# Local attention's weighted sum by accumulating transfers instead of additions on Pool

## The chip, the cores and the metric

The kernel runs on one core of a Trainium2 chip. The core has five engines, each with an instruction queue of its own that runs in order: TensorE (PE), VectorE (DVE), ScalarE (ACT), GpSimd (called Pool here) and SyncE (SP), which in this kernel issues nearly all transfers. They wait for each other by semaphores. The metric is the time of one execution on the device in microseconds (us), median of several runs.

## The reference

The input `x` has 2048 positions of 448 channels, which are 16 heads of 28. Two attentions are computed from it and mixed by a gate per position:

```python
g = _sigmoid((x * gate_w).sum(-1, keepdims=True))
a = _A_ref(x, A_wqkv, A_wo)
b = _B_ref(x, B_wqkv, B_wo)
return g * a + (1 - g) * b
```

B is full softmax attention over all 2048 positions. A is local: each position looks at 8 positions (itself and those 2, 4, ... 14 before it):

```python
W, dil = 8, 2
logits = jnp.einsum("bhsd,bhswd->bhsw", q, kg) * scale
logits = jnp.where(mask[None, None, :, :], logits, -1e9)
attn = _softmax(logits, axis=-1)
o = jnp.einsum("bhsw,bhswd->bhsd", attn, vg)
```

Its last line, a sum of 8 weighted values, is what the change is about. Everything is float32.

## The kernel before

Three stages follow one another. **The projections** (to about 254 us) make queries, keys and values of both attentions and the gate. **The main loop** has 256 steps: 16 units of 16 steps, `st = 16 * u + kt`. A unit is four heads by 512 queries of attention B, a step is 128 of its keys. **The output products** with `wo` begin at step 236 between the last steps and run to the end.

A step of the main loop issues, on TensorE, the scores (line 1022, three products each for accuracy), up to three products for the maxima of a later unit (line 144, until step 234) and the weighted sum of the step before (line 976). ScalarE takes two exponentials (line 1025). VectorE takes two reductions for the maxima (line 148).

**Attention A lies beside this**, in 8 groups of two heads, on VectorE and above all on Pool. A tile is 128 partitions x 896 elements (16 positions x 56 channels), 448 KB. For group `c` and offset `w`:

- `a_score` (line 607): Pool multiplies `q` by the shifted `k` (line 611) into a tile `prod`, and in 40 of 64 cases adds its halves (line 616). `a_reduce` (line 619): VectorE sums each head of it (line 621).
- `a_softmax` (line 623): nine small operations on Pool, VectorE and ScalarE.
- `a_av` (line 653): part 0 multiplies the shifted `v` by the weights (line 661), for `w` = 0 straight into the sum `oat[c]`, else into a tile `prod`; part 1 adds that tile to `oat[c]` (line 666). After the last, `oat[c]` is stored to DRAM (line 669).

The tiles `prod` of scores and of sums come from one pool of five buffers (line 589).

**The order is a list made while the program is written.** `item` puts each operation in a list of its engine with a key (its rank), a cost in us, and needs, each an earlier operation and the number of steps it must lie back. At each step `issue` goes through the list of an engine by rank and issues what has its needs, until `late[eng] + cost` passes a limit, 4.2 us for Pool. `late` falls by 2.25 us a step (2.1 after the maxima end). The engines then run in that order and wait where data is missing. A cost that is too small makes the list issue more than the engine can do.

Other work on Pool is issued by step, not by the list:

- **Maxima.** When a unit's maxima are complete, `max_parts` (line 172) reduces them on VectorE (line 174), copies them on ScalarE and subtracts on Pool (`nmt`, line 181). Two steps later VectorE transposes the result (`nms`, line 186).
- **The end of a unit** (lines 905 to 918), counted from `f = 16 * (u + 1)`: `fin_copy` copies the sums out of PSUM (step f + 1); `fin_sum` and `fin_sum2` bring the softmax sums through DRAM (f + 1, f + 3); `fin_inv` takes the reciprocal on VectorE (line 844) and multiplies it on Pool (line 845, f + 6); `fin_spread` and `fin_spread2` spread it through DRAM as `rbc` (lines 849 and 854, f + 6 and f + 8); `fin_on` multiplies on Pool (line 883, f + 12); `fin_hi` rounds on ScalarE (line 887, f + 15); `fin_lo` subtracts on Pool (line 891, f + 16); `fin_store` stores (f + 19). `pool_time` adds the cost of `fin_on` and `fin_lo` to `late["pool"]`.

When all lists are empty and the last group is stored, `a_done` (line 761) loads `wo` into the room of attention A's tiles and splits it (line 759) over the next thirteen steps.

Of the kernel before, what the change touches and what calls it, by code (L numbers as in the profile page):

```python
# [11 lines left out]
ALU = mybir.AluOpType  # L12
# [8 lines left out]
NU = NG * NB  # L21
# [4 lines left out]
def gated_mix_kernel(ctx: ExitStack, tc: tile.TileContext, xT, xn, gw, wA, wB, woAB, out):  # L26
    nc = tc.nc
# [156 lines left out]
    def max_turn(t):  # L184
        r = sp.tile([128, 32], F32, name="nms")
        nc.vector.transpose(r, t)
        return r
# [18 lines left out]
    with tc.tile_pool(name="xp", bufs=1) as xp, tc.tile_pool(name="wp", bufs=2) as wp:  # L206
# [203 lines left out]
        r, t = xst[:, 0, 0:3, :], xst[:, 0, 3, :]  # L410
# [7 lines left out]
        for kt in range(3):  # L418
            nc.vector.tensor_tensor(out=xl[0][:, kt, :], in0=r[:, kt, :], in1=xh[0][:, kt, :].bitcast(F32),
                                    op=ALU.subtract)  # L420
        nc.vector.tensor_tensor(out=tail[64:128], in0=t[64:128], in1=tail[64:128].bitcast(F32), op=ALU.subtract)
        nc.vector.tensor_tensor(out=wl0[:, 3, 0:256], in0=wt0[:, 0:256], in1=wh0[:, 3, 0:256].bitcast(F32),
                                op=ALU.subtract)
# [27 lines left out]
        for n, t in enumerate(tiles):  # L451
# [4 lines left out]
            for w in splits:  # L456
                i, k = (n - splits[w][0]) * splits[w][1], splits[w][1]
# [36 lines left out]
            if parts and parts[0][0] <= n:  # L494
                _, u, t = parts.pop(0)
                max_store(u, max_turn(t.bitcast(F32)))
            if finished and n < len(tiles) - 3:
                u = finished.pop(0)
                parts.append((n + 3, u, max_parts(u)))
            if n == 64:  # L500
                gate = []
                for sgn, dst in ((-1.0, g_t), (1.0, omg)):
                    e = sp.tile([128, NJ], F32, name="ez")
# [5 lines left out]
            if n == 70:  # L509
                r = max_turn(omw)  # L510
# [10 lines left out]
    def at(pos, st, f):  # L521
        hooks.setdefault((st, pos), []).append(f)
# [12 lines left out]
    pool = ctx.enter_context(tc.tile_pool(name="psv", bufs=1, space=bass.MemoryType.PSUM))  # L535
# [55 lines left out]
    for nme in ("k", "v"):  # L591
        for i in range(2):
            t = a1.tile([128, HALO + NJ, 56], F32, name=f"{nme}t{i}")
            kvt[nme, i] = t
    qt, Lt, oat, lst, prods = {}, {}, {}, {}, {}
# [23 lines left out]
    def a_reduce(c, w, i, n):  # L619
        r = slice(2 * NJ // n * i, 2 * NJ // n * (i + 1))  # L620
        nc.vector.tensor_reduce(Lt[c][:, w].rearrange("p j h -> p (j h)")[:, r], prods[c, w][:, r], axis=X, op=ALU.add)
# [31 lines left out]
    def a_av(c, w, part):  # L653
        if part == 0:
            if w == 0:
                oat[c] = a2.tile([128, NJ, 56], F32, name="oat")
                dst = oat[c]
            else:
                dst = a3.tile([128, NJ, 56], F32, tag="prod", name="prod2")
            oat[c, w] = dst  # L660
            nc.gpsimd.tensor_tensor(  # L661
                out=dst.rearrange("p j (h d) -> p j h d", d=DH),
                in0=kvt["v", c % 2][:, HALO - DIL * w:HALO - DIL * w + NJ, :].rearrange("p j (h d) -> p j h d", d=DH),
                in1=Lt[c][:, w, :, :, None].to_broadcast([128, NJ, 2, DH]), op=ALU.mult)
        else:
            nc.gpsimd.tensor_tensor(out=oat[c], in0=oat[c], in1=oat[c, w], op=ALU.add)  # L666
            if w == W - 1:
                stored[0] = now[0] + 4
                at("end", stored[0], lambda: nc.sync.dma_start(oa_scr[:, :, 56 * c:56 * c + 56], oat[c]))


# [3 lines left out]
    now = [0]  # L675
    stored = [0]

    def item(eng, key, name, cost, needs, f):
        lists[eng].append((key, name, cost, needs, f))

    CH, NR = 21, {}
    for c in range(8):
        for w in range(W):
# [2 lines left out]
    for c in range(8):  # L686
        c0 = CH * c
        for nme in "qkv":
            item("sp", c0 if nme != "v" else c0 + 18, ("ld", nme, c), 0,
                 [(("s", c - 2, 7), 3)] if nme != "v" else [(("a", c - 2, 7, 1), 3)],  # L690
                 lambda c=c, nme=nme: a_load(c, nme))
        for w, o in enumerate((0, 2, 5, 8, 11, 14, 17, 20)):
            back = (c, w - 4) if w > 3 else (c - 1, w + 4)
            item("pool", c0 + o, ("s", c, w), 2.05 + 1.0 * (NR[c, w] == 2),
                 [(("ld", "k", c), 4), (("ld", "q", c), 4), (("a", c - 3, 7, 0), 0), (("s", c, w - 1), 0)]
                 + ([(last(*back), 0)] if back in NR else []), lambda c=c, w=w: a_score(c, w))
            for i in range(NR[c, w]):
                item("dve", c0 + o + 2 + 0.1 * i, ("r", c, w, i), 0.32,
                     [(("s", c, w), 3), (("r", c, w, i - 1) if i else last(c, w - 1) if w else ("r",), 0)],
                     lambda c=c, w=w, i=i: a_reduce(c, w, i, NR[c, w]))  # L700
        for i, (eng, o, cost, lag) in enumerate((("pool", 22, 0.68, 2), ("dve", 23, 0.35, 3), ("dve", 23.5, 0.35, 0),
                                                 ("pool", 25, 0.68, 1), ("act", 26, 0.3, 3), ("dve", 27, 0.35, 1),
                                                 ("dve", 27.5, 0.35, 0), ("dve", 27.8, 0.36, 0),
                                                 ("pool", 28, 0.9, 1))):
            item(eng, c0 + o, ("m", c, i), cost, [(last(c, 7) if i == 0 else ("m", c, i - 1), lag)],
                 lambda c=c, i=i: a_softmax(c, i))
        n = 0
        for w in range(W):
            for part in ((0,) if w == 0 else (0, 1)):
                item("pool", c0 + 30 + 1.4 * n, ("a", c, w, part), 1.65 if part == 0 else 2.05,  # L710
                     [(("m", c, 8), 0), (("ld", "v", c), 4),
                      (("a", c, w - 1, 1 if w > 1 else 0) if part == 0 else ("a", c, w, 0), 0)],
                     lambda c=c, w=w, part=part: a_av(c, w, part))
                n += 1
    for q in lists.values():
# [2 lines left out]
    late = {"pool": 0.0, "dve": 0.0}  # L718
# [109 lines left out]
    fin = {}  # L828
# [13 lines left out]
    def fin_inv(u):  # L842
        r = sp.tile([128, 16], F32, name="finv")
        nc.vector.reciprocal(r, fin["s"])
        nc.gpsimd.tensor_tensor(out=r, in0=r, in1=og[:, u % NB, :], op=ALU.mult)
        fin["rec"] = r
# [50 lines left out]
                r = 112 * g + DH * h  # L897
                dma_r(dst[r:r + DH, 512 * b:512 * b + 512], t[32 * h:32 * h + DH])

    def pool_time(f, *x):  # L900
        late["pool"] += 1.25
        f(*x)


    for u in range(NU - 1):
        f = NJ * (u + 1)
        l = {NU - 3: (1, 2, 5, 6, 9, 12, 13, 15), NU - 2: (1, 2, 5, 6, 8, 10, 10, 12)}.get(
            u, (1, 3, 6, 8, 12, 15, 16, 19))
        at("pre", f + 1, lambda u=u: fin_copy(u))
        at("end", f + l[0], lambda u=u: fin_sum(u))  # L910
        at("end", f + l[1], lambda u=u: fin_sum2(u))
        at("dve", f + l[2], lambda u=u: fin_inv(u))
        at("end", f + l[2], lambda u=u: fin_spread(u))
        at("end", f + l[3], lambda u=u: fin_spread2(u))
        at("end", f + l[4], lambda u=u: pool_time(fin_on, u, fin["r"]))
        at("pre", f + l[5], lambda u=u: fin_hi(u))
        at("end", f + l[6], lambda u=u: pool_time(fin_lo, u, nc.gpsimd))
        at("end", f + l[7], lambda u=u: fin_store(u))


# [20 lines left out]
    part = {}  # L941
# [108 lines left out]
    for u in range(NU):  # L1050
        g, b = divmod(u, NB)
        for kt in range(NJ):
            st = NJ * u + kt
            now[0] = st
            if kt == (8 if u < 12 else 12) and u + 1 < NU:
                load_q(u + 1)
            run("pre", st)
            issue("sp", st, 0)
            if st >= A_START:
                issue("pool", st, 4.2)  # L1060
            if not adone and not any(lists.values()) and st > stored[0]:
                a_done(st)
            cur = {}
            left = s1e - s1c[0]
            for a in scores(u, kt, cur):
                if a == 2:
                    run("mid", st)
            run("dve", st)
            if u and kt == 6:
                late["dve"] += 0.25  # L1070
            if finished:
                v = finished.pop(0)
                t = max_parts(v)
                late["dve"] += 0.3
                turned = {}
                lag = 2 if v < NU - 1 else 1
                at("dve", st + lag, lambda t=t, w=turned: w.update(r=max_turn(t.bitcast(F32))))
                at("end", st + lag, lambda v=v, w=turned: max_store(v, w["r"]))
            issue("dve", st, DLIM)
            issue("act", st, 0)  # L1080
            run("act", st)
            if prev is not None:
                do_av(prev)
            prev = (kt, cur, g)
            if OPS and st >= OPS[0]:
                op_some(st, 7)
            run("end", st)
            step = 2.25 if left else 2.1
            late["dve"] = max(0.0, late["dve"] + 0.58 * min(3, left) - step)
            late["pool"] = max(0.0, late["pool"] - step)  # L1090
            if st == OP0 + 31:
                op_load_b(2, 3)
            if not OPS and s1c[0] == s1e:
                s1_close()
                at("pre", st + 1, lambda: op_t(0))
                at("end", st + 1, lambda: op_split(0))
                OPS.append(st + 2)
# [61 lines left out]
```

## Time and profile before

| | us |
|---|---|
| median of 3 runs | 922.4 (921.13 to 923.32) |
| the profiled execution | 920.4 |
| its span, first to last instruction | 918.4 |
| busy: PE, DVE, ACT, POOL | 905.2, 731.7, 652.5, 620.8 |
| granted TensorE clock | 0.998 |

A row of a group of instructions gives the line, the engine, the operation, output and input tile, their shape, the count; then busy time in total and mean ns of one; then the idle time of the engine just before them and what ended it. A row of the timeline gives start and duration in us, then the instruction, with such an idle time in brackets. "SPq" is the queue of SP that issues transfers. A row of the stages gives start and end, length, the busy time of PE, its weight loads, DVE, ACT and POOL with counts, then clock, the share of the transfer engines, and GB/s.

### The profile page before, as it was taken

What the parts mean: (1) busy time and instruction counts of PE and PEld (TensorE: products, weight loads), DVE (VectorE), ACT (ScalarE), POOL (GpSimd) and SP (SyncE); (2) the same over time, 40 slices, a digit from 0 to 9 for tenths busy, and PEclk for the clock granted to TensorE, in tenths of its full rate; (3) what the DMA queues carried; (4) which work ended last, traced back from release to release, by engine and by line L of the source; (5) the groups of instructions that cost most, each with busy time, mean ns of one, the idle gap of its engine ahead of it and who ended that gap; (6) DMA issues with size and microseconds to landing.
All of it is one profiled execution on the core that took longest, in us unless ns stands there. A gap on an engine that the chain in (4) does not pass through costs nothing.

```text
span 918.4 us, 20670 instructions
## 1 busy us (share of the span) xinstructions
PE 905.2 (99%) x8396; PEld 541.2 (59%) x8396; DVE 731.7 (80%) x977; ACT 652.5 (71%) x802; POOL 620.8 (68%) x485
## 2 busy tenths in 40 slices
PE   8999999999999999999999999999999999999998
PEld 6899999999944444444344444343444444466667
DVE  6488999999989999999889999998999888500012
ACT  6456434433388889898788898888989889855551
POOL 2499746554479799998999999999994851300100
PEclk9999999999999999999999999999999999999999
DMA  9977403544374322235135241531412123453422
GB/s 266 294 254 201 127 11 103 154 120 113 81 245 117 86 81 88 69 91 131 33 117 136 81 102 44 140 93 25 111 44 53 34 63 103 147 161 110 138 82 97
DMA packets 101119, 104.30 MB, mean 114 GB/s; under 512 B 61652, under 2 KB 71252, under 8 KB 100240
## 3 DMA queue, kind: packets, MB, share of 16 engines
q1 hardware_dynamic: 100880, 102.72, 39.4%
q8 instruction: 66, 1.08, 0.5%
q10 hardware_dynamic: 144, 0.26, 0.2%
q14 instruction: 29, 0.24, 0.1%
HBM read 61.99 MB, written 40.48 MB: 112 GB/s over the span
## 4 chain that ended last, share of the span: by engine, by line
PE 76%; POOL 12%; SPq 4%; DMA 4%; ACT 2%; DVE 1%; issue 1%; POOLq 0%; ACTq 0%; DVEq 0%
PE T L1022 20%; PE av L976 18%; PE r L298 14%; PE T L815 8%; PE r L293 7%; PE r L144 5%; POOL prod L611 3%; POOL oat L666 3%; POOL prod L661 3%; SPq L101 2%; PE T L144 2%; DMA rbc<-rs 2%; ACT P L1025 1%; SPq L854 1%; DVE MX L148 1%
## 5 line engine op out<-in xcount | busy, mean ns | idle before, releaser
L1025 ACT ACTIVATE P<-T 128x1024 f32<-128x1024 f32 x512 | 497.2, 1024 | 85.2 <-PE T L1022 83.6
L148 DVE TENSOR_REDUCE MX<-T 128x1 f32<-128x512 f32 x470 | 441.1, 954 | 36.0 <-PE T L144 22.5
L976 PE MATMUL av<-P,V 128*32 128x512 f32 x2048 | 273.6, 606 | 0.0
L1022 PEld LDWEIGHTS T<-QH,KH 30*128 30x128 f32 x1024 | 90.9, 182 | 226.8 <-ACT P L1025 203.3
L144 PE MATMUL T<-KH,QP 28*128 28x512 f32 x704 | 219.3, 453 | 1.4 <-DVE MX L148 1.1
L1022 PE MATMUL T<-QH,KH 30*128 30x512 f32 x1024 | 212.0, 489 | 5.9 <-ACT P L1025 5.0
L162 DVE TENSOR_REDUCE MX<-r 128x2 f32<-128x1024 f32 x160 | 192.6, 1221 | 24.6 <-PE r L144 22.9
L1022 PE MATMUL T<-QH,KL 28*128 28x512 f32 x1024 | 186.5, 397 | 0.0
L1022 PE MATMUL T<-QL,KH 28*128 28x512 f32 x1024 | 184.1, 393 | 0.0
L611 POOL TENSOR_TENSOR prod<-qt,kt 128x896 f32<-128x896 f32 x64 | 135.0, 2113 | 1.4 <-DMA kt<-a_scr 1.4
L362 ACT ACTIVATE raw<-r 128x896 f32<-128x896 f32 (+1 forms) x64 | 58.9, 921 | 97.8 <-PE r L298 96.5
L666 POOL TENSOR_TENSOR oat<-oat,prod 128x896 f32<-128x896 f32 x56 | 118.1, 2109 | 2.3
L144 PEld LDWEIGHTS T<-KH,QP 28*128 28x128 f32 x704 | 86.2, 182 | 28.8 <-ACT P L1025 21.4
L661 POOL TENSOR_TENSOR prod<-vt,L 128x896 f32<-128x896 f32 x56 | 95.4, 1703 | 0.6
L363 POOL TENSOR_TENSOR ast<-raw 128x448 f32<-128x448 f32 x48 | 55.5, 1157 | 58.1 <-ACT raw L362 45.6
L1022 PEld LDWEIGHTS T<-QL,KH 28*128 28x128 f32 x1024 | 93.9, 185 | 0.0
L1022 PEld LDWEIGHTS T<-QH,KL 28*128 28x128 f32 x1024 | 92.2, 183 | 1.0
L144 PE MATMUL r<-KH,QP 64*128 64x512 f32 x320 | 86.7, 390 | 0.0
L976 PEld LDWEIGHTS av<-P,V 128*32 128x32 f32 x2048 | 40.3, 108 | 77.5 <-issue 72.4
L298 PE MATMUL r<-wh,xh 64*128 64x448 f32 (+1 forms) x512 | 85.4, 362 | 0.0
L803 DVE TENSOR_TENSOR oalo<-T,oah 128x384 fp32r<-128x384 f32 x16 | 8.9, 557 | 90.8 <-ACT onhi L802 82.2
L298 PE MATMUL r<-wh,xl 64*128 64x448 f32 (+1 forms) x384 | 70.0, 363 | 0.0
(110 smaller groups left out, 1112.9 us busy)
## 6 DMA issues: line engine op xcount, KB each, us to landing
a_scr<-ast SPq DMA_DIRECT2D x24, 448.0 KB
qk_hi<-qkh SPq DMA_DIRECT2D x24, 256.0 KB
qk_lo<-qkh SPq DMA_DIRECT2D x24, 256.0 KB
rbc<-rs SPq DMA_DIRECT2D x60, 64.0 KB
QP<-qk_hi SPq DMA_DIRECT2D x64, 56.0 KB
KL<-qk_lo SPq DMA_DIRECT2D x16, 224.0 KB
QH<-qk_hi SPq DMA_DIRECT2D x64, 56.0 KB
QL<-qk_lo SPq DMA_DIRECT2D x64, 56.0 KB
```

The lines of the kernel that those rows point to most:

```text
L144: nc.tensor.matmul(bank, qhis[u][h % 2][r, 128 * qs:128 * qs + 128], KH[u // NB % 3][r, 512 * kc:512 * kc + 512], start=True, stop=True)
L148: r = nc.vector.tensor_reduce(MX[:, n % NMX:n % NMX + k], bank, axis=X, op=ALU.max)
L162: nc.vector.tensor_reduce(m, PM[k], axis=X, op=ALU.max)
L293: nc.tensor.matmul(bank, ws[c][rows, k, t[4]:t[4] + 128], x, start=first, stop=last)
L298: nc.tensor.matmul(bank[:, 0:cols], x, ws[c][rows, k, 0:cols], start=first, stop=last)
L611: nc.gpsimd.tensor_tensor(out=p, in0=qt[c], in1=kvt["k", c % 2][:, HALO - DIL * w:HALO - DIL * w + NJ, :], op=ALU.mult)
L661: nc.gpsimd.tensor_tensor(out=dst.rearrange("p j (h d) -> p j h d", d=DH), in0=kvt["v", c % 2][:, HALO - DIL * w:HALO - DIL * w + NJ, :].r ...
L666: nc.gpsimd.tensor_tensor(out=oat[c], in0=oat[c], in1=oat[c, w], op=ALU.add)
L815: writes(bank, nc.tensor.matmul(bank[:, :D], src, wo[c][:, k, :], start=(first and k == ks[0] and i == 0), stop=(last and k == ks[-1] and ...
L976: nc.tensor.matmul(av[32 * h:32 * h + 32, :], V[:, kt, 4 * g + h, :], tiles_[h], start=(kt == 0), stop=(kt == NJ - 1), skip_group_check=True)
L1022: nc.tensor.matmul(bank[a], (KH[g % 3], KH[g % 3], KL[g % 2])[t][r, ks], (qh, ql, qh)[t][r, :], start=(t == 0), stop=(t == 2))
L1025: e = nc.scalar.activation(p, RP[0] if a == "2" else mine, AF.Exp, scale=SCALE).ins
```

## The change

Part 1 of `a_av` no longer adds on Pool: Pool issues a transfer that adds the tile to `oat[c]` on its way from SBUF to SBUF. There are 56 of them. The list gets other costs and needs: a product needs the one before it, and the sum four offsets back issued a step before; a transfer needs its product a step before and the transfer before it three steps before. The store of a group comes 6 steps after its last sum, not 4. `fin_hi`, `fin_lo` and `fin_store` of the first 11 units come three steps later. `finv` and `nmt` now count as Pool time.

```diff
-            nc.gpsimd.tensor_tensor(out=oat[c], in0=oat[c], in1=oat[c, w], op=ALU.add)
+            nc.gpsimd.dma_start(oat[c].rearrange("p j e -> p (j e)"), oat[c, w].rearrange("p j e -> p (j e)"),
+                                accum_op=ALU.add)
             if w == W - 1:
-                stored[0] = now[0] + 4
+                stored[0] = now[0] + 6
                 at("end", stored[0], lambda: nc.sync.dma_start(oa_scr[:, :, 56 * c:56 * c + 56], oat[c]))
...
+    ACC = 1.0
...
-            item("pool", c0 + o, ("s", c, w), 2.05 + 1.0 * (NR[c, w] == 2),
+            item("pool", c0 + o, ("s", c, w), 2.15 + 0.98 * (NR[c, w] == 2),
...
-        for i, (eng, o, cost, lag) in enumerate((("pool", 22, 0.68, 2), ("dve", 23, 0.35, 3), ("dve", 23.5, 0.35, 0),
-                                                 ("pool", 25, 0.68, 1), ("act", 26, 0.3, 3), ("dve", 27, 0.35, 1),
+        for i, (eng, o, cost, lag) in enumerate((("pool", 22, 0.69, 2), ("dve", 23, 0.35, 3), ("dve", 23.5, 0.35, 0),
+                                                 ("pool", 25, 0.69, 1), ("act", 26, 0.3, 3), ("dve", 27, 0.35, 1),
                                                  ("dve", 27.5, 0.35, 0), ("dve", 27.8, 0.36, 0),
-                                                 ("pool", 28, 0.9, 1))):
+                                                 ("pool", 28, 1.14, 1))):
...
-                item("pool", c0 + 30 + 1.4 * n, ("a", c, w, part), 1.65 if part == 0 else 2.05,
+                item("pool", c0 + 30 + 1.4 * n, ("a", c, w, part), 1.72 if part == 0 else ACC,
                      [(("m", c, 8), 0), (("ld", "v", c), 4),
-                      (("a", c, w - 1, 1 if w > 1 else 0) if part == 0 else ("a", c, w, 0), 0)],
+                      (("a", c, w - 1, 0), 0) if part == 0 else (("a", c, w, 0), 1),
+                      (("a", c, w - 4, 1), 1) if part == 0 else (("a", c, w - 1, 1), 3)],
...
-    def pool_time(f, *x):
-        late["pool"] += 1.25
+    def pool_time(t, f, *x):
+        late["pool"] += t
         f(*x)
...
-            u, (1, 3, 6, 8, 12, 15, 16, 19))
+            u, (1, 3, 6, 8, 12, 18, 19, 22) if u < NU - 5 else (1, 3, 6, 8, 12, 15, 16, 19))
...
-        at("dve", f + l[2], lambda u=u: fin_inv(u))
+        at("dve", f + l[2], lambda u=u: pool_time(0.18, fin_inv, u))
...
-        at("end", f + l[4], lambda u=u: pool_time(fin_on, u, fin["r"]))
+        at("end", f + l[4], lambda u=u: pool_time(1.24, fin_on, u, fin["r"]))
...
-        at("end", f + l[6], lambda u=u: pool_time(fin_lo, u, nc.gpsimd))
+        at("end", f + l[6], lambda u=u: pool_time(1.24, fin_lo, u, nc.gpsimd))
...
                 late["dve"] += 0.3
+                late["pool"] += 0.18
```

## The prediction

> **What bounds the kernel now.** I read the page's totals, its 40 slices and its chain first, then placed one instruction that occurs once per unit of 16 steps on the time axis, and then opened the worst stretch instruction by instruction.
>
> ```profile
> PE 905.2 (99%) x8396; PEld 541.2 (59%) x8396; DVE 731.7 (80%) x977; ACT 652.5 (71%) x802; POOL 620.8 (68%) x485
> POOL 2499746554479799998999999999994851300100
> PE 76%; POOL 12%; SPq 4%; DMA 4%; ACT 2%; DVE 1%; issue 1%; POOLq 0%; ACTq 0%; DVEq 0%
> ```
>
> TensorE is busy everywhere and carries the chain. Pool is saturated only in the middle of the span, and it is on the chain for 12%: not because its work is the longest, but because somebody waits for it somewhere. Where, the start of `fin_copy` shows. It is issued at step 1 of each unit; these four belong to steps 17, 65, 161 and 209.
>
> ```profile
> 292.01 0.60 ACT L831 ACTIVATE osb<-av 128x512 f32<-128x512 f32 x1
> 400.21 0.60 ACT L831 ACTIVATE osb<-av 128x512 f32<-128x512 f32 x1
> 625.86 0.60 ACT L831 ACTIVATE osb<-av 128x512 f32<-128x512 f32 x1
> 733.95 0.60 ACT L831 ACTIVATE osb<-av 128x512 f32<-128x512 f32 x1
> ```
>
> Steps 17 to 65 took 108.20 us, 161 to 209 took 108.09 us: 2.253 us a step, twice the same, although Pool adds in both. The 96 steps between took 225.65 us where 96 x 2.253 = 216.3 would do. **So 9.3 us are lost there, and that is all that a faster Pool can win in this loop**; the step itself is set by TensorE, VectorE and ScalarE. The worst of those units, first as Pool and VectorE see it:
>
> ```profile
> 448.06 0.26 DVE L174 TENSOR_REDUCE m<-MX 128x16 f32<-128x64 f32 x1
> 454.98 0.22 POOL L181 TENSOR_TENSOR nmt<-nmv,nmt 128x16 fp32r<-128x16 f32 x1
> 455.23 0.21 DVE L186 STREAM_TRANSPOSE nms<-nmt 128x32 f32<-128x32 f32 x1 [2.47 <-POOL nmt L181]
> 458.05 1.94 ACT L1025 ACTIVATE P<-T 128x1024 f32<-128x1024 f32 x2 [2.67 <-PE T L1022]
> 461.94 1.94 ACT L1025 ACTIVATE P<-T 128x1024 f32<-128x1024 f32 x2 [1.96 <-PE T L1022]
> 464.08 1.94 ACT L1025 ACTIVATE P<-T 128x1024 f32<-128x1024 f32 x2 [0.19 <-PE T L1022]
> 450.38 0.24 DVE L844 RECIPROCAL finv<-fsum 128x16 f32<-128x16 f32 x1
> 457.20 0.21 POOL L845 TENSOR_TENSOR finv<-finv,og 128x16 f32<-128x16 f32 x1
> 465.67 1.82 SPq L854 DMA_DIRECT2D rbc<-rs  x4
> 472.03 1.29 POOL L883 TENSOR_TENSOR on<-osb,rbc 128x512 f32<-128x512 f32 x1 [0.99 <-DMA rbc<-rs]
> 473.35 0.63 ACT L887 ACTIVATE onhi<-on 128x512 fp32r<-128x512 f32 x1 [0.59 <-POOL on L883]
> ACT onhi L887 <- POOL on L883: 4.0, 4, 1.5
> ```
>
> Two mechanisms, both a small Pool instruction queued behind large ones. (1) The maxima are ready at 448.3; Pool's subtraction of 0.22 us runs at 454.98; VectorE, in order, stands 2.47 us at its transpose, and the exponentials then lose 2.67 + 1.96 less twice a normal gap of 0.2 to 0.4: about 4.0 us. (2) Pool's `finv` product comes 6.6 us after the reciprocal, so SP spreads it late, `rbc` lands late, `fin_on` is late, and ScalarE stands before `fin_hi`: 4.0 us in 4 waits of the loop. Together 8 of the 9.3 us; the rest is what follows from them.
>
> **The change part by part.** Pool's prices, by shape:
>
> ```profile
> L611 POOL TENSOR_TENSOR prod<-qt,kt 128x896 f32<-128x896 f32 x64 | 135.0, 2113 | 1.4 <-DMA kt<-a_scr 1.4
> L666 POOL TENSOR_TENSOR oat<-oat,prod 128x896 f32<-128x896 f32 x56 | 118.1, 2109 | 2.3
> L661 POOL TENSOR_TENSOR prod<-vt,L 128x896 f32<-128x896 f32 x56 | 95.4, 1703 | 0.6
> L616 POOL TENSOR_TENSOR prod<-prod 128x448 f32<-128x448 f32 x40 | 41.0, 1025 | 3.1
> L845 POOL TENSOR_TENSOR finv<-finv,og 128x16 f32<-128x16 f32 x15 | 3.4, 224 | 46.6 <-DVE finv L844 46.6
> 300.00:700.00 400.00, 394.16 (x3990) 163.32 (x3984) 377.23 (x572) 349.54 (x395) 383.26 (x258) 1.00 0.32 85
> ```
>
> *Removed*: 56 additions, 118.1 us of a Pool that is busy 383 of 400 us. *Added on Pool*: 56 issues. No Pool issue is in this trace. The nearest row is SP's, below (0.34 us); the far end is 2.1 us, where nothing is saved. I take 1.0, which is what the new list plans (`ACC`), between the ends. That leaves 56 x 1.1 = 62 us less Pool work in the some 450 us of steps 5 to 204, or 14%. The Trainium skill, "DMA: Bandwidth & Descriptors", Latency and other measured facts, gives about 1 us to the first byte on Pool's path against 0.6 on SP's; taken as the price of an issue, an estimate, it would give the same sum. No row here shows it.
>
> *The list's costs.* Before, it counted 2.05, 1.65, 2.05 and 1.0 for the four large rows, nothing for `finv` and `nmt`: short by 64 x 0.063 + 56 x 0.053 + 56 x 0.059 + 40 x 0.025 = 11 us, and with `finv` 14 us, so Pool ran later than the list believed. The new counts (2.15, 1.72, 0.98, `finv` and `nmt` 0.18) come out even with the rows. Worked through with its own numbers, the list issues the last sum of the last group at step 204, before at step 212, and `wo` is loaded and split some six steps earlier: the same seven ScalarE copies and Pool subtractions, ahead of step 236 where the output products begin, so price 0 (were they behind it, each product would wait for its piece). Pool thus has both less to do and a truer list, and I let mechanism (1) go.
>
> *`fin_hi` and `fin_lo` three steps later* for the first 11 units: 3 x 2.253 = 6.8 us more room between `fin_on` and ScalarE, against a longest wait of 1.5 us. Mechanism (2) goes even if Pool stays as late as now. What is late next is `fin_store`, also 3 steps later; its readers come only at step 231. Price 0. The store of a finished group stands on SP and must now wait for the last transfer; it comes 6 steps, 13.5 us, after that is issued, so SP and the loads behind it do not stand.
>
> *The added waits.* A transfer must wait for its product and for the transfer before it (same `oat`), and both waits stand on Pool, with scores, `nmt` and `finv` queued behind; a product of either kind wants one of five `prod` buffers, which a transfer now holds until it lands. The list keeps three steps, 6.76 us, between two transfers of a group. No accumulating transfer is in the trace; its nearest rows:
>
> ```profile
> 781.60 2.13 DMA rs<-finv
> 360.85 0.34 SPq L604 DMA_DIRECT2D vt<-a_scr  x1
> 361.23 0.43 SPq L605 DMA_DIRECT2D vt<-a_scr  x1
> GB/s 0 0 0 0 0 0 0 31 188 188 125 63 125 220 282 251 314 408 376 408 345 421 403 479 462 287 466 430 430 287 502 394 287 215 143 36 200 0 0 0
> 424.72 6.49 DMA rbc<-rs
> 467.07 4.80 DMA rbc<-rs
> ```
>
> 8 KB take 2.13 us, nearly all of it fixed. The two `vt` loads (448 and 392 KB; the GB/s row is 361 to 365 us in slices of 0.1 us) move 840 KB from 361.7 to 364.7: 448 KB in about 1.6 us. An accumulation reads source and target, so one to two times that: 2.13 + 1.6 to 3.2, plus 1.0 of issue, is 4.7 to 6.3 us. The upper end from afar is `rbc`, which took 6.49 us in a crowd. I take 5.5, below 6.76: a few waits where Pool issues one transfer late and the next on time, no standing delay. For those I leave 1.5 us of stall (bounds 0 and the 9.3 of today; nearest row, the 2.47 us of VectorE's wait).
>
> **Sum.** The profiled execution took 920.4 us (span 918.4 and 2.0 around it). 920.4 - 9.3 + 1.5 = 912.6. The median of the runs shown, 922.4, is 2.0 above that execution, so 914.6 for a median.
>
> **Rivals.**
>
> *A. The transfer is longer than three steps (slower).* Place: the wait for the previous sum, on Pool. If issue to landing is x, each of the 8 x 6 = 48 gaps between sums of a group becomes x, and nothing else runs on Pool meanwhile, so the loop is paced by it: 48 (x - 6.76). It decides from x = 6.76 and is back at today's time at about 6.95; x = 7.3 costs 26 us, 939. For it: the 6.49 us row, and an arithmetic rate that no row shows. Against: the 4.7 to 6.3 above. 16%.
>
> *B. The issue is not cheap (slower).* From about 1.5 us an issue Pool is again later than the list believes, by 28 us over the 56, of which I let half reach TensorE: 922.4 - 9.3 + 14 = 927. At 2.1 us the list is wrong by 62 us: 944. For it: Pool does in software what SP does in 0.34 us. 8%.
>
> *C. The wait moves (no change).* Pool's lateness before `fin_on` is partly SP's and the transfers': in the row above `rbc` took 6.49 us behind K loads. 56 transfers of 448 KB, at 3.2 us each, take 179 us of all queues' time in about 450 us, a share of 0.4 beside today's 0.32. If `rbc` and the `prod` buffers then hold Pool as long as its additions did, `nmt` is as late as now, only `fin_hi` gains, and buffer waits give that back: 921 to 924. The Trainium skill speaks for this in "DMA: Bandwidth & Descriptors", Issuing engines are not separate DMA queues: transfers of all issuers share the same 16 engines. The trace agrees so far that crowded transfers take longer (6.49 against 4.80 us for the same four). 10%.
>
> *D. Half of it.* As C, but `fin_hi` keeps its gain of 4 to 5 us: 917 to 920. 12%.
>
> **How the numbers follow.** Forecast 54% (912 to 917 as medians), D 12%: faster 0.66. C: same 0.10. A and B: slower 0.24. A difference under 0.2%, 1.8 us, is about what a measurement here cannot tell from none. Lowest: all 9.3 us go and nothing comes, 911.1 in the execution, with the fastest run (921.13) as offset 911.8, and a little for ScalarE's own order: 911. The top has to leave out no more than the bad half of A and B: 930.
>
> **What would show it.** Right: `fin_copy` from step 65 to 161 in 216 to 219 us; no wait of ScalarE's `fin_hi` for Pool; VectorE's transpose never over 1 us behind `nmt`; Pool issues of about 1 us, and Pool at 80 to 85% between 300 and 700 us instead of 96%. Wrong: waits of Pool for its own transfers in a large sum (A), issues of 1.5 us and more (B), `rbc` as the releaser of `fin_on` in most units (C).

## The result: slower by 9.2%

| | before | after |
|---|---|---|
| median of 5 runs, us | 922.64 (921.13 to 923.32) | 1007.74 (1005.31 to 1009.53) |
| ratio after to before | | 1.0922, 95% interval 1.0903 to 1.0942 |
| span of the profiled execution, us | 918.4 | 1005.4 |
| mean granted TensorE clock of that execution | 0.998 | 0.956 |

The forecast was 914.6 us, the range 911 to 930. The page of the kernel after (its totals, the clock in 40 slices, the chain by engine and by line):

```profile
PE 937.0 (93%) x8396; PEld 549.5 (55%) x8396; DVE 733.1 (73%) x977; ACT 653.1 (65%) x802; POOL 552.6 (55%) x485
PEclk9999999999999988997799978979979999999999
PE 54%; POOL 19%; DMA 16%; issue 4%; SPq 3%; ACT 2%; DVE 2%; POOLq 0%; ACTq 0%; DVEq 0%
DMA oat<-prod 15%; PE r L298 13%; PE T L1025 10%; PE av L979 10%; POOL prod L611 8%; PE T L818 7%; PE r L293 7%; POOL prod L661 5%; PE r L144 4%; POOL prod L616 2%; SPq L101 2%; ACT P L1028 2%; PE T L144 1%; POOL oat L661 1%; DVE MX L148 1%
```

Pool's busy time fell as the change meant it to, from 620.8 to 552.6 us. But the new transfers, `oat<-prod`, are on the chain with 15%, and Pool has 19% in place of 12%. TensorE does the same 8396 matmuls in 937.0 us instead of 905.2, which is 31.8 us more; the other 55 of the 87 us by which the span grew are time in which it does nothing. Pool's groups, by shape (from line 713 on, the lines of the kernel after stand three higher than before):

```profile
L611 POOL TENSOR_TENSOR prod<-qt,kt 128x896 f32<-128x896 f32 x64 | 139.0, 2174 | 59.8 <-DMA oat<-prod 51.2 <-DVE MX L148 4.0 <-DVE L L621 2.7
L661 POOL TENSOR_TENSOR prod<-vt,L 128x896 f32<-128x896 f32 x56 | 98.1, 1768 | 55.7 <-DMA oat<-prod 55.5
L666 POOL DMA_DIRECT2D oat<-prod x56 | 48.9, 878 | 21.4 <-DMA oat<-prod 17.3 <-ACT P L1028 2.8 <-POOL prod L661 0.9
```

An issue costs 0.88 us where the addition cost 2.11: 118.1 - 48.9 = 69 us less work. The last part of each row is what was paid: 51.2 + 55.5 = 107 us in which a *product* waits for a transfer, 17.3 us in which a transfer waits for a transfer, 124 us in all. A product reads nothing that a transfer writes. It waits for the `prod` buffer that the transfer still reads. The list of waits of the kernel after, in us, times, longest, shows who waits for Pool in turn:

```profile
POOL prod L661 <- DMA oat<-prod: 55.5, 18, 7.7
DVE L L621 <- POOL prod L611: 32.4, 6, 9.1
DVE nms L186 <- POOL nmt L181: 25.7, 4, 9.0
```

`nmt`, whose lateness the change was to end, is now late by up to 9.0 us. Where the time goes along the steps, by the same instruction as in the prediction, `fin_copy` at steps 65, 161 and 209:

```profile
416.75 0.60 ACT L834 ACTIVATE osb<-av 128x512 f32<-128x512 f32 x1
694.35 0.60 ACT L834 ACTIVATE osb<-av 128x512 f32<-128x512 f32 x1
820.28 0.60 ACT L834 ACTIVATE osb<-av 128x512 f32<-128x512 f32 x1
```

Up to step 65 the kernel has lost 416.75 - 400.21 = 16.5 us, from 65 to 161 it takes 277.6 us where before took 225.65, from 161 to 209 125.9 where before took 108.1: 16.5 + 52.0 + 17.8 = 86 us, all of it while local attention runs. One of those stalls, in the timeline of the kernel after, engine by engine:

```profile
445.99 0.85 POOL L666 DMA_DIRECT2D oat<-prod  x1
454.55 1.69 POOL L661 TENSOR_TENSOR prod<-vt,L 128x896 f32<-128x896 f32 x1 [7.71 <-DMA oat<-prod]
456.21 1.25 POOL L886 TENSOR_TENSOR on<-osb,rbc 128x512 f32<-128x512 f32 x1
457.49 0.60 ACT L834 ACTIVATE osb<-av 128x512 f32<-128x512 f32 x1 [4.59 <-POOL on L886]
459.53 0.68 DVE L621 TENSOR_REDUCE L<-prod 128x8 f32<-128x224 f32 x2 [6.96 <-POOL prod L611]
451.24 1.06 PE L979 MATMUL av<-P,V 128*32 128x512 f32 x8
458.14 1.94 PE L979 MATMUL av<-P,V 128*32 128x512 f32 x8 [4.54 <-ACT osb L834]
463.57 1.93 PE L979 MATMUL av<-P,V 128*32 128x512 f32 x8
467.33 1.07 PE L979 MATMUL av<-P,V 128*32 128x512 f32 x8
```

Read it from the top. Pool issues a transfer and wants to go on with the next product. That product's buffer is the one just given to the transfer, so Pool stands 7.71 us. Behind it is `fin_on`, which reads `osb`; ScalarE may not overwrite `osb` before that, and stands 4.59 us; TensorE's next eight `av` matmuls wait for ScalarE, 4.54 us; VectorE waits 6.96 us for the score product behind `fin_on`. And it is not over when the work resumes: eight `av` matmuls that take 1.06 us take 1.94 and 1.93 us before they are back at 1.07. The windows of the same kernel around it (start and end, length, busy PE, PEld, DVE, ACT, POOL, then the clock, the share of the transfer engines, GB/s) say why:

```profile
440.00:452.00 12.00, 12.00 (x125) 4.78 (x123) 11.39 (x17) 10.53 (x12) 6.68 (x6) 1.00 0.93 211
452.00:458.00 6.00, 1.60 (x19) 0.80 (x15) 0.57 (x1) 1.41 (x3) 3.45 (x3) 0.91 0.48 76
458.00:463.00 5.00, 4.45 (x21) 1.61 (x23) 3.30 (x6) 2.58 (x5) 4.03 (x3) 0.50 0.50 95
463.00:468.00 5.00, 5.00 (x37) 1.54 (x31) 2.77 (x4) 2.66 (x3) 4.21 (x4) 0.59 0.24 49
468.00:472.00 4.00, 4.00 (x46) 1.84 (x46) 4.00 (x8) 3.38 (x5) 1.85 (x1) 1.00 1.01 297
```

Behind 4.5 us without matmuls the granted clock is 0.50, then 0.59 in the mean, and 1.00 from 468 us. In windows of 0.5 and 1 us of the same trace, TensorE's last matmul before the stall ends at 453.6, the clock is 1.00 until 456.5, 0.50 from 457 to 467, and 1.00 from 468. So a long stall is paid twice: by standing, and by the slow matmuls behind it. The Trainium skill, "TensorE: Matmul & The Clock Gate", What's actually happening, has it that the clock is halved after an idle window of about 3.4 us and comes back after as long a busy one. These rows agree with the half and with the idle time. The return took longer here, some 9 us from the first matmul, and TensorE was busy without a pause only from 462 on.

### The profile page after: what moved, and what is told of

It is laid out like the page before. It is cut to its first block, busy times and chain, and to the rows that moved or that the text cites. A ratio compares the mean times of both kernels' runs of the same rounds, so it can differ in the third digit from the quotient of the medians.

```text
span 1005.4 us, 20735 instructions
## 1 busy us (share of the span) xinstructions
PE 937.0 (93%) x8396; PEld 549.5 (55%) x8396; DVE 733.1 (73%) x977; ACT 653.1 (65%) x802; POOL 552.6 (55%) x485
## 4 chain that ended last, share of the span: by engine, by line
PE 54%; POOL 19%; DMA 16%; issue 4%; SPq 3%; ACT 2%; DVE 2%; POOLq 0%; ACTq 0%; DVEq 0%
DMA oat<-prod 15%; PE r L298 13%; PE T L1025 10%; PE av L979 10%; POOL prod L611 8%; PE T L818 7%; PE r L293 7%; POOL prod L661 5%; PE r L144 4%; POOL prod L616 2%; SPq L101 2%; ACT P L1028 2%; PE T L144 1%; POOL oat L661 1%; DVE MX L148 1%
## 5 line engine op out<-in xcount | busy, mean ns | idle before, releaser
L979 PE MATMUL av<-P,V 128*32 128x512 f32 x2048 | 283.8, 627 | 4.7 <-ACT osb L834 4.5
L144 PE MATMUL T<-KH,QP 28*128 28x512 f32 x704 | 227.1, 468 | 48.9 <-DVE MX L148 48.5
L1025 PE MATMUL T<-QH,KH 30*128 30x512 f32 x1024 | 219.1, 504 | 8.8 <-DVE MX L148 7.2
L1025 PE MATMUL T<-QH,KL 28*128 28x512 f32 x1024 | 193.8, 413 | 0.0
L1025 PE MATMUL T<-QL,KH 28*128 28x512 f32 x1024 | 191.4, 409 | 0.0
L611 POOL TENSOR_TENSOR prod<-qt,kt 128x896 f32<-128x896 f32 x64 | 139.0, 2174 | 59.8 <-DMA oat<-prod 51.2
L144 PEld LDWEIGHTS T<-KH,QP 28*128 28x128 f32 x704 | 90.0, 190 | 79.1 <-DVE MX L148 52.9
L661 POOL TENSOR_TENSOR prod<-vt,L 128x896 f32<-128x896 f32 x56 | 98.1, 1768 | 55.7 <-DMA oat<-prod 55.5
L1025 PEld LDWEIGHTS T<-QL,KH 28*128 28x128 f32 x1024 | 97.9, 194 | 0.0
L1025 PEld LDWEIGHTS T<-QH,KL 28*128 28x128 f32 x1024 | 96.0, 191 | 2.8
L621 DVE TENSOR_REDUCE L<-prod 128x16 f32<-128x224 f32 (+1 forms) x176 | 61.9, 374 | 46.7 <-POOL prod L611 32.4
L363 POOL TENSOR_TENSOR ast<-raw 128x448 f32<-128x448 f32 x48 | 55.5, 1155 | 58.2 <-ACT raw L362 45.7
```

Of the source, the lines that this page charges most:

```text
L144: nc.tensor.matmul(bank, qhis[u][h % 2][r, 128 * qs:128 * qs + 128], KH[u // NB % 3][r, 512 * kc:512 * kc + 512], start=True, stop=True)
L611: nc.gpsimd.tensor_tensor(out=p, in0=qt[c], in1=kvt["k", c % 2][:, HALO - DIL * w:HALO - DIL * w + NJ, :], op=ALU.mult)
L661: nc.gpsimd.tensor_tensor(out=dst.rearrange("p j (h d) -> p j h d", d=DH), in0=kvt["v", c % 2][:, HALO - DIL * w:HALO - DIL * w + NJ, :].r ...
L979: nc.tensor.matmul(av[32 * h:32 * h + 32, :], V[:, kt, 4 * g + h, :], tiles_[h], start=(kt == 0), stop=(kt == NJ - 1), skip_group_check=True)
L1025: nc.tensor.matmul(bank[a], (KH[g % 3], KH[g % 3], KL[g % 2])[t][r, ks], (qh, ql, qh)[t][r, :], start=(t == 0), stop=(t == 2))
```

## The experiments

**Theory 1**: the five `prod` buffers. In the program, 45 of the 120 products carry a wait on a transfer, and in 41 of them the buffer that comes free is the one that the transfer issued last reads. **Rivals**: the length of the transfer itself (three steps between two sums are too few), the price of an issue, the traffic of the transfers, and the list's new order.

**More buffers.** Ten buffers need memory, so the eight tiles of exponentials were cut to four; the first kernel has that cut alone.

```diff
-    probs = [ep.tile([128, 2, 512], F32, name=f"P{i}") for i in range(8)]
+    probs = [ep.tile([128, 2, 512], F32, name=f"P{i}") for i in range(4)]
...
-    a3 = actx.enter_context(tc.tile_pool(name="a3", bufs=5))
+    a3 = actx.enter_context(tc.tile_pool(name="a3", bufs=7))
```

Four tiles, five buffers:

> The changed kernel with 4 instead of 8 tiles P for the exponentials, five prod buffers as before. It makes room and changes nothing else: a P tile's readers are, in TensorE's order, already behind it when the fourth exponential after it is taken. Both theories: 1000 to 1015 us, as the changed kernel (1007.7). Another time would mean that the P tiles count, and that the next two are to be read against this one.

Four tiles, seven buffers:

> The same with seven prod buffers. Theory 1 (Pool's products wait for a buffer that a transfer issued just before still holds until it lands): the 107 us in which products wait for transfers fall below 25 us, and the time to 912 to 925 us. Theory 2 (the transfers themselves are too slow for three steps, so that one waits for the one before): Pool's transfer issues take over the wait, 50 us and more, and the time stays above 980 us.

Four tiles, ten buffers:

> The same with ten prod buffers. Theory 1: a product waits for no transfer that it can feel, 911 to 918 us, at most 5 us below seven buffers. Theory 2: as with seven, above 980 us. If some 20 us of waits of transfers for transfers are left but the time is near 913, these waits are harmless.

With five buffers 1006.7 us (one run), as the kernel after: the cut costs nothing there. With seven 919.7 us, ratio to before 0.9981 (0.9969 to 0.9993); with ten 919.6, ratio 0.9978 (0.9962 to 0.9994). Two more buffers take away 87 us, and the waits of products on transfers fall from 107 to 0.7 us:

```profile
POOL prod L661 <- DMA oat<-prod: 0.7, 2, 0.4
```

With ten buffers there are none. In the program, 12 products carry a wait on a transfer with seven buffers and 6 with ten, none of these 6 on the transfer issued last. So the buffers are the cause of the loss. But both kernels stand just below before, and ten buffers miss the 911 to 918 that the theory gave them. What was still waited for with ten buffers, and Pool's groups there:

```profile
POOL on L886 <- DMA rbc<-rs: 38.3, 9, 18.6
POOL oat L666 <- DMA oat<-prod: 29.3, 12, 4.3
```

```profile
L611 POOL TENSOR_TENSOR prod<-qt,kt 128x896 f32<-128x896 f32 x64 | 148.2, 2317 | 1.9 <-DMA kt<-a_scr 1.9
L666 POOL DMA_DIRECT2D oat<-prod x56 | 53.0, 956 | 35.7 <-DMA oat<-prod 29.3 <-DMA nm<-nms 4.2 <-POOL prod L661 1.2
```

**The transfer shorter, and the transfer a plain copy**, both with five buffers, one run each. The first leaves out 15/16 of each addition, the second all of it.

```diff
-            nc.gpsimd.dma_start(oat[c].rearrange("p j e -> p (j e)"), oat[c, w].rearrange("p j e -> p (j e)"),
-                                accum_op=ALU.add)
+            nc.gpsimd.dma_start(oat[c].rearrange("p j e -> p (j e)")[:, 0:56], oat[c, w].rearrange("p j e -> p (j e)")[:, 0:56],
+                                accum_op=ALU.add)
```

> The changed kernel, five buffers, but each transfer adds only the first 56 of 896 columns (the rest of the sum is left out). Same issues, same order, same buffers; only the landing is shorter, some 2.5 us for 4.9. Theory 1 and 2 both expect a large gain, since both hang on the landing: 925 to 950 us. If it stays near 1000, neither the buffers' nor the transfers' wait on data movement is the cause, but the issues or the order of the list.

942.1 us; products still wait 23.0 + 19.7 us. A sixteenth of the bytes does not set a buffer free at once: these transfers land 2.4 us after their issue in the median, not 4.9.

```diff
-            nc.gpsimd.dma_start(oat[c].rearrange("p j e -> p (j e)"), oat[c, w].rearrange("p j e -> p (j e)"),
-                                accum_op=ALU.add)
+            nc.gpsimd.dma_start(oat[c].rearrange("p j e -> p (j e)"), oat[c, w].rearrange("p j e -> p (j e)"))
```

> The changed kernel with plain copies in place of accumulating transfers (the sum is left out, the last copy wins); order, buffers and waits as in the change. If the arithmetic in the transfer is what makes landings long, the median landing falls from 4.9 to some 3.5 us and the time to 940 to 970; if not, 4.5 to 4.9 us and 990 to 1010.

961.7 us, products wait 38.2 + 37.0 us. The row of the page for the issues (KB, median us from issue to landing), first of the kernel after, then of the copy, and the copy's issues on Pool:

```profile
oat<-prod POOLq DMA_DIRECT2D x56, 448.0 KB, 4.9
```

```profile
oat<-prod POOLq DMA_DIRECT2D x56, 448.0 KB, 3.3
```

```profile
L666 POOL DMA_DIRECT2D oat<-prod x56 | 32.3, 577 | 9.2 <-DMA oat<-prod 7.7 <-POOL prod L661 0.9 <-POOL finv L847 0.3
```

An accumulating transfer of 448 KB lands after 4.9 us, a copying one after 3.3, and its issue takes 0.88 against 0.58 us. Where the landing is a third shorter, the products' waits are too: 75 us instead of 107.

**The list and the late `fin_hi` without the transfers.** Pool adds as before, and the needs of products and sums and the 4 steps to a group's store are those of before too; the rest of the change stays. The list counts 2.12 for an addition (measured: 2.11).

```diff
-            nc.gpsimd.dma_start(oat[c].rearrange("p j e -> p (j e)"), oat[c, w].rearrange("p j e -> p (j e)"),
-                                accum_op=ALU.add)
+            nc.gpsimd.tensor_tensor(out=oat[c], in0=oat[c], in1=oat[c, w], op=ALU.add)
...
-    ACC = 1.0
+    ACC = 2.12
...
-                      (("a", c, w - 1, 0), 0) if part == 0 else (("a", c, w, 0), 1),
-                      (("a", c, w - 4, 1), 1) if part == 0 else (("a", c, w - 1, 1), 3)],
+                      (("a", c, w - 1, 1 if w > 1 else 0) if part == 0 else ("a", c, w, 0), 0)],
```

> The additions are back on Pool, and all else of the change stays: the list's measured costs (an addition counted 2.12), fin_hi, fin_lo and fin_store three steps later; the needs of products and sums and the 4 steps to the store are those of before. If the stall of before (9.3 us between steps 65 and 161) comes from a list that counts too little and from the place of fin_hi, as the prediction had it: 912 to 917 us, without any transfer. If it comes from Pool's amount of work: 919 to 924.

913.92 us (912.85 to 914.16), ratio 0.9909 (0.9897 to 0.9922): **faster than both kernels**, with Pool as busy as it ever was. `fin_copy` at steps 65 and 161, and the window from 300 to 700 us:

```profile
401.04 0.61 ACT L832 ACTIVATE osb<-av 128x512 f32<-128x512 f32 x1
617.75 0.61 ACT L832 ACTIVATE osb<-av 128x512 f32<-128x512 f32 x1
```

```profile
300.00:700.00 400.00, 399.87 (x4075) 166.11 (x4071) 383.69 (x579) 356.26 (x402) 378.80 (x254) 1.00 0.32 86
```

216.7 us for the 96 steps, where the undisturbed step asks for 216.3. TensorE is busy 399.87 of 400 us while Pool is busy 378.80: a Pool at 95% costs nothing, as long as its small, urgent instructions come in time.

**The late `fin_hi` alone**, on the kernel before.

```diff
-            u, (1, 3, 6, 8, 12, 15, 16, 19))
+            u, (1, 3, 6, 8, 12, 18, 19, 22) if u < NU - 5 else (1, 3, 6, 8, 12, 15, 16, 19))
```

> The kernel before with only fin_hi, fin_lo and fin_store of the first 11 units three steps later. By the prediction's mechanism 2, ScalarE's 4.0 us of waits for Pool go and the 4.0 us of mechanism 1 stay: 917 to 919 us. If the wait only moves to fin_lo or to a later product: 921 to 923.

919.07 us, ratio 0.9975 (0.9964 to 0.9987): 2.3 of the 8.4 us that the list and the late `fin_hi` win together. The larger part comes only when the list's measured costs are there too. The costs without the late `fin_hi` were not run, and which of them does it is not shown.

**What keeps ten buffers 5.7 us behind that.** Two waits were in sight: `fin_on` for `rbc`, and a transfer for the one before it. Each was given more room, with ten buffers and four tiles.

```diff
-            u, (1, 3, 6, 8, 12, 18, 19, 22) if u < NU - 5 else (1, 3, 6, 8, 12, 15, 16, 19))
+            u, (1, 3, 6, 8, 15, 18, 19, 22) if u < NU - 5 else (1, 3, 6, 8, 12, 15, 16, 19))
```

> Ten product buffers with four P tiles as before, and fin_on placed three steps later (15 instead of 12 after its unit). The run with ten buffers stood at 919.6 us, the kernel with Pool's own additions and the new list at 913.9. Theory 1: those 6 us come from Pool standing at fin_on, because the accumulating transfers make rbc late (38.3 us of waits on rbc there); then the waits on rbc outside the last units go and the time is 914 to 917. Theory 2: they come from a transfer that waits for the one before it (29.3 us); then nothing changes here, 918.5 to 920.5.

```diff
-                      (("a", c, w - 4, 1), 1) if part == 0 else (("a", c, w - 1, 1), 3)],
+                      (("a", c, w - 4, 1), 1) if part == 0 else (("a", c, w - 1, 1), 4)],
```

> Ten product buffers with four P tiles as before, and the list keeps two transfers of a tile four steps apart instead of three. Theory 1 (rbc late): waits of a transfer for the one before fall from 29 us to under 10, but the time stays at 918.5 to 920.5. Theory 2 (transfer waits for transfer): 914 to 917.

Both theories fell, each by the run that gave it room. `fin_on` three steps later made 922.96 us, ratio 1.0023 (1.0013 to 1.0033): the waits on `rbc` inside the loop are gone, but Pool then stands at a transfer, and `fin_on` is so close to the next unit's `fin_copy` that ScalarE stands behind it. Its timeline:

```profile
436.44 0.88 POOL L666 DMA_DIRECT2D oat<-prod  x1 [5.18 <-DMA oat<-prod]
442.54 1.26 POOL L886 TENSOR_TENSOR on<-osb,rbc 128x512 f32<-128x512 f32 x1
443.84 0.60 ACT L834 ACTIVATE osb<-av 128x512 f32<-128x512 f32 x1 [4.75 <-POOL on L886]
```

Four steps between transfers made 919.15 us, ratio 0.9975 (0.996 to 0.9991), as with three. Its waits:

```profile
POOL on L886 <- DMA rbc<-rs: 56.7, 10, 18.8
POOL oat L666 <- DMA oat<-prod: 11.0, 7, 3.6
```

These rows also hold waits behind local attention. Up to 720 us, four steps have 30.5 us of waits on `rbc` and 11.0 of a transfer for another, three steps had 13.7 and 29.3: 41.5 against 43.0, so the wait mostly moved from one transfer to the other. That pointed to what both wait for. In the stretch where this happens the transfer engines are full; two windows of the kernel with ten buffers, and the chain's piece for one transfer in the kernel with the late `fin_on`:

```profile
424.00:428.00 4.00, 4.00 (x46) 1.72 (x38) 3.89 (x7) 3.39 (x5) 3.21 (x3) 1.00 0.98 207
428.00:432.00 4.00, 4.00 (x42) 1.67 (x42) 3.92 (x6) 3.70 (x4) 0.35 (x1) 1.00 1.03 193
```

```profile
427.02 8.89 DMA oat<-prod
```

There a transfer takes 8.89 us instead of 4.9. So two last kernels: ten buffers with the short transfer of above, and a control that gives the kernel with Pool's own additions four tiles.

```diff
-            nc.gpsimd.dma_start(oat[c].rearrange("p j e -> p (j e)"), oat[c, w].rearrange("p j e -> p (j e)"),
+            nc.gpsimd.dma_start(oat[c].rearrange("p j e -> p (j e)")[:, 0:56], oat[c, w].rearrange("p j e -> p (j e)")[:, 0:56],
```

> Ten product buffers, four P tiles, and transfers that carry 56 of the 896 columns, so that 15/16 of each addition is left out; Pool's issues, their places and the waits stay. Traffic theory (between 420 and 440 us the DMA engines are full, share about 1.0 for some 8 us, so a transfer lands after 6.6 to 9.2 us instead of 4.9 and rbc comes up to 6 us late; Pool meets whichever it reaches first): 912 to 915, with no step over 3.5 us in units 0 to 13 and no waits of a transfer for another. Issue theory (what is left is the 0.9 us of an issue and the longer product behind it): 917 to 920.

> The kernel with Pool's own additions and the new list (913.9 us) with four P tiles in place of eight, to see whether the room for the ten buffers has a price of its own where nothing else stalls. If it has none: 913 to 915. If the four P tiles are the 6 us by which the ten-buffer kernels stay behind: 918 to 920.

The control took 913.93 us, ratio 0.9912 (0.9897 to 0.9926): four tiles have no price. The short transfers with ten buffers took 914.22 us, ratio 0.9918 (0.9904 to 0.9931). `fin_copy` at steps 65 and 161 there:

```profile
400.45 0.60 ACT L834 ACTIVATE osb<-av 128x512 f32<-128x512 f32 x1
617.47 0.61 ACT L834 ACTIVATE osb<-av 128x512 f32<-128x512 f32 x1
```

217.0 us, and waits of a transfer for another of 2.9 us. So the bytes of the transfers are what ten buffers still pay for, 919.6 - 914.2 = 5.4 us; the issues are not. The Trainium skill, "DMA: Bandwidth & Descriptors", Issuing engines are not separate DMA queues, says that transfers interleave on the same 16 engines whoever issues them. The runs agree: the share of these engines from 300 to 700 us is 0.65 with full transfers and 0.38 with short ones, and the K, V and `rbc` loads of SP are in the same crowd. One wait on `rbc` stays in this stretch with short transfers too (2.84 against 4.44 us), and costs nothing there.

**A list that knows of five buffers**, with the eight tiles as in the kernel after.

```diff
...
+            b = ring[-5]
+            d, lag = (last(b[1], b[2]), 1) if b[0] == "s" else (("a", b[1], b[2], 1), 3)
+            if issued.get(d, 10 ** 6) + lag > st:
+                return True
...
-            if any(d in names and issued.get(d, 10 ** 6) + lag > st for d, lag in needs):
+            if any(d in names and issued.get(d, 10 ** 6) + lag > st for d, lag in needs) or eng == "pool" and held(name, st):
...
```

> The changed kernel with its five product buffers and eight P tiles; only the list is changed: a product is not issued before the transfer that read its buffer was issued three steps earlier, or before the last reduction of that buffer was issued one step earlier. By an emulation of the list all of Pool's work then ends at step 220 instead of 211, with 234 as the end of the steps. Theory of the buffers: the waits of products on transfers fall from 107 us to under 15, the time is 917 to 925, near that with seven buffers (919.7). Rival, that five buffers are too few in whatever order: over 35 us of such waits and over 940 us.

939.72 us, ratio 1.0194 (1.0169 to 1.0219). The waits:

```profile
POOL prod L661 <- DMA oat<-prod: 37.2, 14, 4.8
POOL oat L666 <- DMA oat<-prod: 24.1, 11, 4.4
POOL prod L611 <- DMA oat<-prod: 20.8, 8, 5.0
```

68 of the 85 us come back with an order alone, but products still wait 58.0 us, and transfers 24.1 us for each other. That is far from the under 15 of the theory and close to the rival, five buffers too few in whatever order (over 35 us of waits, over 940 us). Yet the run does not decide between them, because its rule looks at the wrong buffer. It takes the five to go round (`ring[-5]`), but in the program 78 of the 115 later products get another buffer than that of the fifth product before them. So 32 products still carry a wait on a transfer, 29 of them on the one issued last. A list that keeps track of the true buffers was not tried.

## Why the prediction was wrong

The step that failed is the last one of *The added waits*. It says that "a product of either kind wants one of five `prod` buffers, which a transfer now holds until it lands". But the only term that follows is for transfers that come too close: "a few waits where Pool issues one transfer late and the next on time, no standing delay. For those I leave 1.5 us of stall". The wait of a product for its buffer was named and got no price of its own, and no reason for that is given. It cost 87 us (1006.7 with five buffers, 919.7 with seven). It could have been counted. The list was worked through for the ends of its chains, but not for how many buffers are wanted at a time: by its own steps up to seven, if a transfer holds its buffer for the three steps that the list leaves it, where there are five. A product then mostly gets the buffer of the transfer issued last, and its wait is what is left of that transfer's landing, again and again, not once. Nearly all else of the miss is the 5.4 us that the bytes of the transfers cost, which the sum had at nothing: 914.6 + 87 + 5.4 = 1007.0, measured 1007.7.

Point by point:

- *What bounds the kernel*, 9.3 us lost between steps 65 and 161 and nothing else for a faster Pool to win: right. The additions with the new list lose 0.4 us there, and win 8.4 us in all by the ratio. That also says that the 62 us of Pool work that the transfers were to save were not needed: short transfers with ten buffers have Pool busy 343 of 400 us and are no faster than the additions at 379.
- *The issue at 1.0 us* (0.34 to 2.1): 0.88 measured, right. Rival B, an issue of 1.5 us and more, is false. What the sum lacked is that the product behind an issue becomes longer (below), some 0.2 us each; it costs no time in the run with short transfers.
- *The landing at 5.5 us from the issue* (4.7 to 6.3): 4.9 as the median, right, but 8.89 in the crowd above. Rival A put the loss at a transfer that waits for the one before; that wait is only 17.3 of the 124 us. Its sign, a large sum of waits of Pool for its own transfers, did come, but by another way: what mostly waited for the landing was a product that wanted the buffer.
- *Mechanism (2) goes with the late `fin_hi`*: right, but alone it wins 2.3 us, not the 4.0 of its waits.
- *Mechanism (1) goes because the list is truer*: right with Pool's own additions, where the time came out as forecast (913.9, forecast 914.6), for another kernel than the one forecast. With the transfers and five buffers `nmt` is later than ever, and with ten VectorE waits 3.8 us for it, as before.
- *Rival C* had the buffers beside `rbc` as what "then hold[s] Pool as long as its additions did", at no change. Right in kind, far too small: it let the wait be as long as the work that went (69 us), and it became 124, on an engine whose waits TensorE shares. That the clock halves behind a long stall, with 31.8 us more of matmul time in all, was in no term.
- *The chances*: 0.24 for slower came from A and B, neither of which happened.

## What to carry to other kernels

When an engine's work is handed to a transfer, the buffer that it reads is no longer free when the engine has passed, but when the transfer lands: count the buffers that are held in that time against those there are, before anything else is priced. If the next instruction of the same queue allocates from the same ring, its wait is the whole landing, and whatever stands behind it on that engine is late by as much. And ask first whether the saved work was in the way: here a plan with the measured durations won 8.4 us with all the work still on Pool.

## What the runs showed of the hardware

- An accumulating transfer between tiles of SBUF, 448 KB, takes 0.88 us of Pool to issue and 4.9 us to land; the same transfer as a copy 0.58 and 3.3. The Trainium skill, "DMA: Bandwidth & Descriptors", Anatomy of one DMA, gives a fit of 2.0 us plus the bytes at 436 GB/s, by which 448 KB would be an estimate of 3.05 us. The copy comes near it, the accumulation doesn't.
- The product that Pool runs behind an accumulating issue is longer. In the kernel after, 15 score products that start directly behind an issue took 2.35 to 2.40 us, and 6 that first stood waiting behind one 2.06 to 2.11; directly behind a copy's issue they took 2.08 to 2.13. In the kernel with ten buffers all score products take 2317 ns in the mean (row above). With Pool's own additions, with ten buffers and short transfers (a sixteenth of the bytes), and with copies the rows are:

```profile
L611 POOL TENSOR_TENSOR prod<-qt,kt 128x896 f32<-128x896 f32 x64 | 135.3, 2117 | 1.2 <-DMA kt<-a_scr 1.2
L611 POOL TENSOR_TENSOR prod<-qt,kt 128x896 f32<-128x896 f32 x64 | 148.1, 2315 | 1.7 <-DMA kt<-a_scr 1.7
L611 POOL TENSOR_TENSOR prod<-qt,kt 128x896 f32<-128x896 f32 x64 | 134.9, 2109 | 43.1 <-DMA oat<-prod 38.2 <-DVE L L621 2.7 <-DMA kt<-a_scr 1.9
```

  So it goes with the issue of an accumulating transfer, not with its bytes; why is open.
- In the stall shown above, of 4.5 us, TensorE's clock stood at 0.50 from 457 to 467 us, and some 9 us of that lay behind the stall; there the same eight matmuls took 1.94 instead of 1.06 us.
